# A scale vector computed by rows of matmuls instead of column tiles, behind four parked blocks

## The chip, the cores and the metric

The kernel runs on one core of a Trainium2 chip. The metric is device time in microseconds (us). The core has five engines that run side by side and wait for each other: TensorE (PE in the profile, its weight loads PEld), VectorE (DVE), ScalarE (ACT), GpSimd (POOL), and SyncE (SP), which here only issues transfers. Matmul results go to PSUM, which the kernel uses as eight banks of 128 partitions x 512 words; all else lies in SBUF.

## The reference

The reference is one attention block with adaptive layer norm, for 2 batches of 256 tokens of width 1152, in bfloat16:

```python
mod = (_silu(c) @ w_mod).reshape(B, 6, 1, D)
shift_a, scale_a, gate_a, shift_m, scale_m, gate_m = [mod[:, i] for i in range(6)]
h = _layernorm(x, axis=-1) * (1 + scale_a) + shift_a
qkv = h @ wqkv
q, k, v = qkv[..., :D], qkv[..., D:2 * D], qkv[..., 2 * D:]
p = _softmax(jnp.einsum('bqd,bkd->bqk', q, k) * D ** (-0.5), axis=-1)
a = jnp.einsum('bqk,bkd->bqd', p, v) @ wo
return x + gate_a * a
```

The change concerns `1 + scale_a`: for each of the two batches a vector of 1152 numbers, silu(c) times the columns of w_mod that belong to scale_a, and 1.

## The kernel before

The 512 tokens are four tiles of 128 (`TT`); the width is nine blocks of 128 (`KT`). The kernel centres the tokens (`centre`), turns each tile on PE so that the width lies on the partitions (`turn_firsts` for the first two of the nine blocks, into one bank; `turn_rest` for the other seven, copied to `xcT`), multiplies each block k by its part of `1 + scale_a` (`hTs`, one DVE instruction for each batch of 256 tokens), and feeds it to the K projection. The 1/std of each token is put in later, on the projected result, so the K matmuls need the scale and not the variance.

The scale vector is computed in four parts, `PA` (blocks 0, 1), `PB` (2, 3, 4), `PC` (5, 6) and `PD` (7, 8), as their weights `wS` arrive. Three of the parts are computed by rows (`scale_rows`): for each block and each of nine slices of c, one matmul with a 128x128 weight tile of `wS` and 32 columns, which are the two batches repeated; the sums fall on the partitions, where the scaling needs them. `PB` is computed by tiles (`scale_tiles`): silu(c) is the weight, 32 columns wide, and `wS` streams past; four such matmuls use four quarters of the array. The sums then lie along a row of 32 partitions, and a DVE transpose in blocks of 32 (`scale_turned`) puts them on the partitions, into `sT`. `PA` and `PB` are opened by a matmul of one row of ones (`scale_open`), which puts the 1 of `1 + scale_a` into the sum; `PC` and `PD` have it added by a DVE instruction (`scale_out`, into `s1p`).

The K projection has nine output blocks. Five of them collect in five banks (`accs`, ring `MM`) while blocks k = 0 to 8 come in (`k_row`, `k_step`; `k_row` takes some outputs in halves of 256 tokens, as the first half is scaled first). The other four, the parked ones, first take only k = 0 and 1 (`park_part`, two matmuls of 512 columns each) and are copied to `held` (`park`, on ACT or DVE); the rest is collected later (`held_block`) and added. The parked blocks, the scale parts and other small things share the three single banks `BA`, `BB`, `BC`; whoever takes a bank waits until the one before has been read out.

Each engine runs its instructions in the order in which the program writes them (`pin`). Around the change PE's order before is: the turns of tiles 0 and 1; `PA` rows for slices 0 to 3; the turn of tile 2; the first two turns of tile 3; `PA` rows for slices 4 to 8; the other turns of tile 3; K rows 0 and 1; parked block 0 (bank BA); the opening of `PB` (BC) and its tiles for slices 0 to 3; parked block 1 (BB); the tiles for slices 4 to 8; parked blocks 2 (BA) and 3 (BB); K rows 2, 3, 4. DVE in that time scales blocks 0 and 1, takes the statistics of tile 3 (`bn_part` three times and `bn_aggr`), copies parked block 1, transposes the `PB` sums and scales blocks 2, 3 and 4. ACT takes the squares of tiles 1 and 2 (`act_var`) and copies parked blocks 0, 2 and 3. POOL then makes 1/std from all four tiles' variances (`rstd`), in seven steps, and PE transposes the result (`pT3`) among the later K rows.

All instructions are recorded by one helper, so the profile gives nearly all of them line 85; they are told apart by the names of their tiles: `psS` is a scale part, `psE` a parked block, `acc` one of the five collecting banks, `tpA` and `tp` the turns, `psK` the rest of the parked blocks, `psQ` the Q projection, `ps` values, attention and output.

Of the kernel before, what the change touches and what calls it, by code (L numbers as in the profile page):

```python
# [8 lines left out]
ALU = mybir.AluOpType  # L9
AX = mybir.AxisListType  # L10
F32 = mybir.dt.float32
BF16 = mybir.dt.bfloat16
# [4 lines left out]
def kernel(  # L17
# [10 lines left out]
    P = 128  # L28
    B, N, D = x.shape
    T = B * N  # L30
    KT = D // P
# [3 lines left out]
    NCH = D // CW  # L35
# [5 lines left out]
    PA, PB, PC, PD = (0, 2), (2, 5), (5, 7), (7, KT)  # L41
    KA = PA[1]
    NR = 32
# [12 lines left out]
    const = ctx.enter_context(tc.tile_pool(name="const", bufs=1))  # L56
# [5 lines left out]
    MM, BA, BB, BC = (psum, "mm"), (psum_a, "pa"), (psum_b, "pb"), (psum_c, "pc")  # L62
# [3 lines left out]
    def bank(shape, name, dtype=None, where=None):  # L66
        if where is None:
            where = ring[turn_no[0] % len(ring)]
            turn_no[0] += 1
        return where[0].tile(shape, dtype or F32, tag=where[1], name=name)  # L70
# [21 lines left out]
    vec = _Rec(nc.vector, dve_seq)  # L92
    sca = _Rec(nc.scalar, act_seq)
    ten = _Rec(nc.tensor, pe_seq)
    spq = _Rec(nc.sync, sp_seq)
    gps = _Rec(nc.gpsimd, pool_seq)
# [10 lines left out]
    def tok(b):  # L107
        return slice(b * N, (b + 1) * N)

    def one(t):  # L110
        return slice(t * P, (t + 1) * P)

    junk = const.tile([P, 512], BF16)
# [4 lines left out]
        out=ident, in_=ident, compare_op=ALU.not_equal, fill=1.0, base=0,  # L118
# [8 lines left out]
        out=mask, in_=mask, compare_op=ALU.is_ge, fill=0.0, base=0,  # L127
# [3 lines left out]
        out=mask, in_=mask, compare_op=ALU.is_ge, fill=0.0, base=2,  # L131
# [2 lines left out]

    c_sb = const.tile([P, B, KT], BF16)
    x_sb = act.tile([P, TT, D], BF16)
    ones_row = const.tile([1, (PB[1] - PB[0]) * NR], BF16)
    gps.memset(ones_row, 1.0)
    sca.preload_act_table_set("natural_log_exp_and_others")
    sca.dma_start(out=c_sb, in_=c.rearrange("b (p k) -> p b k", k=KT))  # L140
# [4 lines left out]
    wS = wmpool.tile([P, KT, D], BF16, tag="wS")  # L145
# [60 lines left out]
    def sc_rhs(kk):  # L206
        return scT_rep[:, kk].rearrange("p r b -> p (r b)")
# [8 lines left out]
    mvs = const.tile([P, TT, 2], F32)  # L216
    snm = const.tile([P, TT], F32)
    rstd = const.tile([P, TT], F32)
    nmean = const.tile([P, TT], F32)
# [3 lines left out]
    def bn_part(t, st, s):  # L223
        vec.bn_stats(out=st[:, s, :], in_=x_sb[:, t, s * CW : (s + 1) * CW])
# [9 lines left out]
    def act_mean(t):  # L234
        sca.activation(out=xc[:, t, :], in_=x_sb[:, t, :], func=ACT.Copy, scale=-1.0 / D,
                       accum_out=nmean[:, t : t + 1])

    def act_var(t):
        sca.activation(out=xc[:, t, :], in_=x_sb[:, t, :], func=ACT.Square, bias=snm[:, t : t + 1],
                       scale=float(D) ** -0.5, accum_out=mvs[:, t, 1:2])  # L240

    def centre(t, scalar, op, c0=0, c1=D):
        vec.tensor_scalar(out=xc[:, t, c0:c1], in0=x_sb[:, t, c0:c1], scalar1=scalar, scalar2=None, op0=op)
# [5 lines left out]
    def turn_firsts(t):  # L249
        for k in range(KA):  # L250
            ten.transpose(firsts[:, k, t, :], xc[:, t, k * P : (k + 1) * P], ident)

    def turn_rest(t, where):
        rests[t] = bank([P, KT - KA, P], "tp", BF16, where)
        for k in range(KA, KT):
            ten.transpose(rests[t][:, k - KA, :], xc[:, t, k * P : (k + 1) * P], ident)

    def copy_rest(t, on_dve=False):
        evac(on_dve, xcT[:, KA:KT, one(t)], rests[t])

    def evac(on_dve, out_ap, in_ap):
        if on_dve:
            return vec.tensor_copy(out=out_ap, in_=in_ap)
        return sca.copy(out=out_ap, in_=in_ap)
# [8 lines left out]
    psS = {}  # L273

    def scale_open(part, where):
        n = part[1] - part[0]
        psS[part] = bank([P, n, NR], "psS", where=where)
        ten.matmul(psS[part].rearrange("p j r -> p (j r)"), lhsT=junk[0:1, :P], rhs=ones_row[0:1, 0 : n * NR],
                   start=True, stop=False, skip_group_check=True)

    def scale_rows(part, kk0, kk1, js=None, where=None):
        opened = part == PA
        if kk0 == 0 and not opened:
            psS[part] = bank([P, part[1] - part[0], NR], "psS", where=where)
        for j0, j1 in [part] if js is None else js:
            for kk in range(kk0, kk1):
                for j in range(j0, j1):
                    ten.matmul(psS[part][:, j - part[0], :], lhsT=wS[:, kk, j * P : (j + 1) * P], rhs=sc_rhs(kk),
                               start=(kk == 0 and j == part[0] and not opened), stop=(kk == KT - 1),
                               skip_group_check=True)  # L290

    def scale_out(part):
        vec.tensor_scalar_add(out=s1p[:, part[0] : part[1], :], in0=psS[part][:, :, 0:B], scalar1=1.0)


    wS_v = wS.rearrange("p kk (k j c) -> p kk k j c", k=KT, j=4)
    sT = const.tile([P, KT, 32], F32)

    def scale_tiles(part, kk0, kk1):
        for kk in range(kk0, kk1):  # L300
            for j in range(4):
                ten.matmul(psS[part][32 * j : 32 * j + 32], lhsT=sc_rhs(kk), rhs=wS_v[:, kk, part[0] : part[1], j, :],
                           start=False, stop=(kk == KT - 1), skip_group_check=True)

    def scale_turned(part):
        vec.transpose(out=sT[:, part[0] : part[1], :].rearrange("p k c -> p (k c)"),
                      in_=psS[part].rearrange("p k c -> p (k c)"))

    def scaled(k, sl, scalar):
        vec.tensor_scalar(out=hTs[:, k, sl], in0=xcT[:, k, sl], scalar1=scalar, scalar2=None, op0=ALU.mult)  # L310
# [6 lines left out]
    def scaled_b(k, b):  # L317
        scaled(k, tok(b), s1p[:, k, b : b + 1])

    def wk(k, f):  # L320
        return wK[:, k, f * P : (f + 1) * P]
# [8 lines left out]
    def park_part(i, where):  # L330
        parked[i] = bank([P, T], "psE", where=where)
        for k in range(KA):
            ten.matmul(parked[i], lhsT=wk(k, NACC + i), rhs=hTs[:, k, :], start=(k == 0), stop=(k == KA - 1))

    def park(i, on_dve=False):
        evac(on_dve, held[:, i, :], parked[i])
# [8 lines left out]
    def held_block(i, rows, where=None):  # L345
        if where is not None:
            psK[i] = bank([P, T], "psK", where=where)
        for k in range(*rows):
            ten.matmul(psK[i], lhsT=wk(k, NACC + i), rhs=hTs[:, k, :], start=(k == KA), stop=(k == KT - 1))
# [16 lines left out]
    sca.activation(out=xc[:, 2, 0:SPLIT], in_=x_sb[:, 2, 0:SPLIT], func=ACT.Copy, accum_out=half_a)  # L366
    vec.reduce_sum(out=half_v, in_=x_sb[:, 2, SPLIT:D], axis=AX.X)
    vec.tensor_scalar(out=nmean[:, 2:3], in0=half_v, scalar1=half_a, scalar2=-1.0 / D, op0=ALU.add, op1=ALU.mult)
    centre(2, nmean[:, 2:3], ALU.add)
    act_mean(3)  # L370
    gps.tensor_scalar_mul(out=snm[:, 1:3], in0=nmean[:, 1:3], scalar1=float(D) ** -0.5)
    for c0, c1 in ((0, KA * P), (KA * P, D)):
# [6 lines left out]
    turn_firsts(2)  # L379
    turn_rest(2, BB)  # L380
    copy_rest(2)
    turn_firsts(3)
    scale_rows(PA, 4, KT)
    turn_rest(3, BC)
    for b in range(B):
        scaled_first(0, b, psS[PA][:, 0, b : b + 1])
# [7 lines left out]
    def k_row(k, by_batch):  # L394
        for b in range(B):
            k_part(k, tok(b), 0, by_batch)
        k_part(k, slice(0, T), by_batch, NACC)
# [2 lines left out]
    k_row(1, 0)  # L400
    act_var(1)
    st3 = small.tile([P, NCH, 6], F32, tag="stats", name="stats")
    for i in range(NCH):
        bn_part(3, st3, i)
    vec.bn_aggr(out=mvs[:, 3, :], in_=st3)
    park_part(0, BA)
    park(0)
    scale_open(PB, BC)
    scale_tiles(PB, 0, 4)
    park_part(1, BB)  # L410
    park(1, on_dve=True)
    scale_tiles(PB, 4, KT)
    scale_turned(PB)
    for k in range(*PB):
        for b in range(B):
            scaled(k, tok(b), sT[:, k, b : b + 1])
    act_var(2)
    park_part(2, BA)
    park(2)
    park_part(3, BB)  # L420
    park(3)
    parts_sq = const.tile([P, P], BF16)
    gps.memset(parts_sq, 0.0)
    parts = parts_sq[:, 0 : 3 * TT].rearrange("p (t i) -> p t i", i=3)
# [8 lines left out]

    def scale_part(part):
        scale_rows(part, 0, KT, where=BB)
        scale_out(part)
        for k in range(*part):
            for b in range(B):  # L440
                scaled_b(k, b)

    k_row(PB[0], 2)
    for k in range(PB[0] + 1, PB[1]):
        k_step(k)
    held_block(0, (2, 4), BA)
    scale_part(PC)
    held_block(0, (4, 5))
    held_block(1, PB, BC)
    k_step(5)  # L450
# [4 lines left out]
    held_block(0, (5, 6))  # L455
    held_block(1, (5, 6))
    k_step(6, 0, 2)
    scale_part(PD)
    k_step(6, 2, NACC)
    bc_ps = bank([P, T], "bc_ps", where=BB)  # L460
    ten.matmul(bc_ps, lhsT=junk[:, :P], rhs=masked.rearrange("p t n -> p (t n)"), start=True, stop=True)
# [103 lines left out]
    for b in range(B):  # L565
        s_ps = bank([P, NQ, N], "s_ps")
        for i in range(NQ):
            tq = b * NQ + i
            for k in range(KT):
                ten.matmul(s_ps[:, i, :], lhsT=qkT[:, k, tq * P : (tq + 1) * P], rhs=qkT[:, KT + k, tok(b)],  # L570
                           start=(k == 0), stop=(k == KT - 1))
# [75 lines left out]
    for b in range(B):  # L647
        for gi, dv0 in enumerate(range(0, KT, 2)):
            ndv = min(2, KT - dv0)
            ps = bank([P, 2, N], "ps")  # L650
            for dd in range(ndv):
                dv = dv0 + dd
                for j in range(NQ):
                    ten.matmul(ps[:, dd, :], lhsT=v_sb[:, b * NQ + j, dv * P : (dv + 1) * P],
                               rhs=pT_sbs[b][:, j, :], start=(j == 0), stop=(j == NQ - 1))
# [3 lines left out]
    for t in range(TT):  # L659
        b = t // NQ  # L660
# [4 lines left out]
        else:  # L665
            chunks, c0 = [], 0
# [4 lines left out]
        for ci, (c0, w_) in enumerate(chunks):  # L671
# [6 lines left out]
            for k in range(KT):  # L678
                ten.matmul(
                    ps, lhsT=attnT[:, k, t * P : (t + 1) * P],  # L680
                    rhs=(wo_last[:, k, c0 - (D - TAILW) : c0 - (D - TAILW) + w_] if pregated else wO[:, k, cs]),
                    start=(k == 0 and not pregated), stop=(k == KT - 1),
# [49 lines left out]
```

## Time and profile before

| | |
|---|---|
| time, median of 3 runs | 96.34 us (96.31 to 96.38) |
| the profiled execution | 96.41 us |
| its span, first to last instruction | 94.6 us |
| PE busy | 90.1 us, 95% of the span |
| DVE busy | 69.1 us, 73% |
| ACT busy | 33.8 us, 36% |
| POOL busy | 20.8 us, 22% |
| the chain that ended last | PE 92%, DVE 4% |
| granted clock of TensorE | 1.0 |

A row of the timeline has the start and the length in us, the engine, the operation, the tiles it writes and reads, its shape, and the count of equal instructions that follow each other; in brackets stands the idle time of the engine before it and what ended it. For a matmul the first pair of numbers is the part of the array that it uses (128\*32 is 128 rows and 32 columns), then comes the shape of the data that stream past. Matmuls overlap, so a row of n matmuls lasts longer than the next one's start tells: what counts is the distance of starts. In the chain, each piece goes from the end of the one before to its own end.

### The profile page before, as it was taken

The numbers are of one execution on the slowest core, as the hardware profiler recorded it, in microseconds if no ns is written. First come the engines' busy times: TensorE is split into PE (matmuls) and PEld (weight loads), VectorE is DVE, ScalarE is ACT, GpSimd is POOL, SyncE is SP. The second block draws the span as 40 slices with busy tenths as digits, with TensorE's granted clock in tenths as the row PEclk, the third lists the DMA queues.
The fourth block names the chain that finished last, engine by engine and source line by source line (L and its number), as shares of the span: only waits on it lengthen the run. The fifth ranks groups of instructions, "written<-read, shape, count | busy, mean of one in ns | idle before, by whom it ended". The sixth has DMA issues, their size and how long they took to land.

```text
span 94.6 us, 1638 instructions
## 1 busy us (share of the span) xinstructions
PE 90.1 (95%) x641; PEld 51.7 (55%) x641; DVE 69.1 (73%) x128; ACT 33.8 (36%) x68; POOL 20.8 (22%) x26
## 2 busy tenths in 40 slices
PE   3999999999999999999999999999999999999970
PEld 1349544545445444444468656566578656565660
DVE  2497966045897999999997899990018587889880
ACT  5189975001561720093420588234246300000010
POOL 5623007200000000000000000008999990002000
PEclk9999999999999999999999999999999999999999
DMA  2999999999999999999999502200000000312212
GB/s 24 341 291 370 377 394 359 376 410 411 413 399 406 412 408 415 397 372 373 386 401 413 233 1 55 49 7 7 0 0 0 0 0 0 125 44 88 115 46 88
DMA packets 17232, 21.31 MB, mean 225 GB/s; under 512 B 2249, under 2 KB 10569, under 8 KB 17225
## 3 DMA queue, kind: packets, MB, share of 16 engines
q1 hardware_dynamic: 16809, 21.17, 61.8%
q8 instruction: 5, 0.08, 0.4%
q10 hardware_dynamic: 416, 0.04, 0.3%
q14 instruction: 2, 0.02, 0.0%
HBM read 19.76 MB, written 1.18 MB: 221 GB/s over the span
## 4 chain that ended last, share of the span: by engine, by line
PE 92%; DVE 4%; issue 0%
PE ps L85 38%; PE psQ L85 18%; PE acc L85 11%; PE psK L85 7%; PE junk_ps L85 5%; PE s_ps L85 4%; PE psS L85 2%; PE psE L85 2%; DVE o_sb L85 2%; PE tp L85 2%; DVE ga L85 2%; PE psH L85 1%; PE tpA L85 1%; DVE junk L85 1%; DVE hTs L85 0%
## 5 line engine op out<-in xcount | busy, mean ns | idle before, releaser
L85 POOL PARTITION_ALL_REDUCE gate_bc<-gacc x2 | 13.7, 6888 | 47.1 <-DVE gacc L85 47.1
L85 DVE SCALAR_TENSOR_TENSOR gacc<-wG,scT_f,gacc 128x1152 f32<-128x1152 bf16 x16 | 22.4, 1416 | 0.4
L85 PE MATMUL ps<-wV,hT 128*128 128x384 bf16 x108 | 17.7, 326 | 0.0
L85 PE MATMUL psQ<-hT,wQ 128*128 128x512 bf16 x81 | 17.6, 379 | 0.0
L85 PE MATMUL ps<-wO,attnT 128*128 128x384 bf16 (+3 forms) x108 | 17.2, 322 | 0.0
L85 PEld LDWEIGHTS <-attnT 128*128 128x128 bf16 x117 | 11.1, 98 | 6.5
L85 PEld LDWEIGHTS <-hT 128*128 128x128 bf16 x108 | 10.6, 98 | 6.9
L85 PEld LDWEIGHTS <-wQ 128*128 128x128 bf16 x81 | 7.9, 98 | 9.6
L85 PEld LDWEIGHTS <-wK 128*128 128x128 bf16 x85 | 7.8, 97 | 8.6 <-issue 1.1
L85 PE MATMUL acc<-hTs,wK 128*128 128x512 bf16 (+1 forms) x49 | 10.7, 361 | 0.0
L85 ACT CAST qkT<-psQ 128x512 bf16<-128x512 f32 x9 | 4.9, 596 | 10.6 <-PE psQ L85 10.6
L85 DVE TENSOR_TENSOR ga<-ps,gate_bc 128x384 f32<-128x384 f32 (+3 forms) x12 | 6.5, 545 | 2.8 <-PE ps L85 2.7
L85 DVE CAST attnT<-ps 128x512 bf16<-128x512 f32 (+1 forms) x6 | 3.5, 603 | 6.8 <-PE ps L85 6.8
L85 ACT CAST v_sb<-ps 128x384 bf16<-128x384 f32 x12 | 5.5, 476 | 7.9 <-PE ps L85 7.9
L85 PE MATMUL psK<-hTs,wK 128*128 128x512 bf16 x28 | 7.0, 379 | 0.0
L85 DVE TENSOR_TENSOR o_sb<-ga,x_sb 128x384 bf16<-128x384 f32 (+3 forms) x12 | 6.6, 547 | 0.4
L85 ACT CAST o_sb<-ps 128x128 bf16<-128x128 f32 x1 | 0.3, 267 | 17.3 <-PE ps L85 17.3
L85 PE MATMUL junk_ps<-junk 128*128 128x512 bf16 x11 | 4.9, 632 | 1.5 <-DVE junk L85 1.5
L85 DVE TENSOR_TENSOR hT<-hTs,held 128x512 bf16<-128x512 bf16 x9 | 5.7, 683 | 0.4 <-ACT held L85 0.4
L85 PEld LDWEIGHTS <-junk 128*128 128x128 bf16 (+1 forms) x14 | 1.8, 133 | 5.4 <-issue 3.7
L85 DVE BATCH_NORM_STATS2 stats<-x_sb 128x6 f32<-128x384 bf16 x6 | 3.0, 541 | 2.3 <-DMA x_sb<-in_x_dram 2.3
L85 PE MATMUL s_ps<-qkT 128*128 128x256 bf16 x36 | 4.1, 272 | 0.0
(82 smaller groups left out, 84.9 us busy)
## 6 DMA issues: line engine op xcount, KB each, us to landing
wG<-in_w_mod_dram SPq DMA_DIRECT2D x3, 864.0 KB, 12.0
wV<-in_wqkv_dram SPq DMA_DIRECT2D x3, 864.0 KB, 13.4
wO<-in_wo_dram SPq DMA_DIRECT2D x3, 864.0 KB, 9.0
wH<-in_w_mod_dram SPq DMA_DIRECT2D x2, 1152.0 KB, 9.5
wQ<-in_wqkv_dram SPq DMA_DIRECT2D x4, 576.0 KB, 11.7
wK<-in_wqkv_dram SPq DMA_DIRECT2D x7, 288.0 KB, 6.2
wS<-in_w_mod_dram SPq DMA_DIRECT2D x3, 320.0 KB, 6.6
x_sb<-in_x_dram SPq DMA_DIRECT2D x3, 288.0 KB, 3.4
```

The source lines that it names most:

```text
L85: r = fn(*a, **k)
```

## The change

`PB` is now computed by rows as well, and as a whole behind the four parked blocks. Its first block (2) stands alone in bank BB, opened by a matmul of the whole 128x128 array (128 rows of ones against 1/128), and is scaled straight from PSUM. Blocks 3 and 4 follow in bank BC without an opening; `scale_out` adds 1 and writes `s1p`. Parked block 2 goes to bank BC and parked block 3 to BA. ACT copies parked block 2 before it takes the squares of tile 2. DVE's third statistic of tile 3 and the aggregation stand behind the scaling of blocks 3 and 4. The centring of tile 2 is cut in two at column 512. The `PA` rows for slices 4 to 8 stand ahead of the first two turns of tile 3.

```diff
-    ones_row = const.tile([1, (PB[1] - PB[0]) * NR], BF16)
+    ones_row = const.tile([1, 2 * NR], BF16)
...
+    ones_part = const.tile([P, NR], BF16)
+    gps.memset(ones_part, 1.0 / P)
+
+    def scale_open_one(part, where):
+        psS[part] = bank([P, 1, NR], "psS", where=where)
+        ten.matmul(psS[part][:, 0, :], lhsT=junk[:, :P], rhs=ones_part, start=True, stop=False, skip_group_check=True)
+
     def scale_rows(part, kk0, kk1, js=None, where=None):
-        opened = part == PA
+        opened = part in psS
...
-    wS_v = wS.rearrange("p kk (k j c) -> p kk k j c", k=KT, j=4)
-    sT = const.tile([P, KT, 32], F32)
-
-    def scale_tiles(part, kk0, kk1):
-        for kk in range(kk0, kk1):
-            for j in range(4):
-                ten.matmul(psS[part][32 * j : 32 * j + 32], lhsT=sc_rhs(kk), rhs=wS_v[:, kk, part[0] : part[1], j, :],
-                           start=False, stop=(kk == KT - 1), skip_group_check=True)
-
-    def scale_turned(part):
-        vec.transpose(out=sT[:, part[0] : part[1], :].rearrange("p k c -> p (k c)"),
-                      in_=psS[part].rearrange("p k c -> p (k c)"))
...
-    centre(2, nmean[:, 2:3], ALU.add)
+    for c0, c1 in ((0, 4 * P), (4 * P, D)):
+        centre(2, nmean[:, 2:3], ALU.add, c0, c1)
...
+    scale_rows(PA, 4, KT)
     turn_firsts(3)
-    scale_rows(PA, 4, KT)
...
-    for i in range(NCH):
-        bn_part(3, st3, i)
-    vec.bn_aggr(out=mvs[:, 3, :], in_=st3)
+    bn_part(3, st3, 0)
+    bn_part(3, st3, 1)
+
+    def scale_part(part, where):
+        scale_rows(part, 0, KT, where=where)
+        scale_out(part)
+        for k in range(*part):
+            for b in range(B):
+                scaled_b(k, b)
+
     park_part(0, BA)
     park(0)
-    scale_open(PB, BC)
-    scale_tiles(PB, 0, 4)
     park_part(1, BB)
     park(1, on_dve=True)
-    scale_tiles(PB, 4, KT)
-    scale_turned(PB)
-    for k in range(*PB):
-        for b in range(B):
-            scaled(k, tok(b), sT[:, k, b : b + 1])
+    park_part(2, BC)
+    park(2)
     act_var(2)
-    park_part(2, BA)
-    park(2)
-    park_part(3, BB)
+    park_part(3, BA)
     park(3)
+    PB1, PB2 = (PB[0], PB[0] + 1), (PB[0] + 1, PB[1])
+    scale_open_one(PB1, BB)
+    scale_rows(PB1, 0, KT)
+    for b in range(B):
+        scaled(PB[0], tok(b), psS[PB1][:, 0, b : b + 1])
+    scale_part(PB2, BC)
+    bn_part(3, st3, 2)
+    vec.bn_aggr(out=mvs[:, 3, :], in_=st3)
...
-    scale_part(PC)
+    scale_part(PC, BB)
```

## The prediction

> **What bounds the kernel now.** I read the page first, then the chain that ended last, then the waits, and then the order of time around the edit. From the page come the span and the shares of the chain:
>
> ```profile
> span 94.6 us, 1638 instructions
> PE 92%; DVE 4%; issue 0%
> ```
>
> The chain in order of time (start, us, what) lies on the matrix engine, PE, from about 9.7 to 88.9; its longest pieces are:
>
> ```profile
> 31.13 17.48 PE psQ L85 x81
> 48.61 3.93 PE s_ps L85 x36
> 52.54 36.36 PE ps L85 x234
> ```
>
> The 81 psQ matmuls of 512 columns advance by 17.48/81 = 0.216 us each. Eight such parked matmuls (psE) need 8 x 0.216 = 1.73 us. The stretch that is changed, from the first psE matmul to the first acc matmul of row 2, is in the timeline of PE (start, us, operation):
>
> ```profile
> 11.89 0.59 PE L85 MATMUL psE<-hTs,wK 128*128 128x512 bf16 x2
> 12.42 0.21 PE L85 MATMUL psS<-ones_row,junk 1*128 1x96 bf16 x1
> 12.56 0.35 PE L85 MATMUL psS<-wS,scT_rep 128*32 128x96 bf16 x16
> 12.85 0.60 PE L85 MATMUL psE<-hTs,wK 128*128 128x512 bf16 x2
> 13.38 0.40 PE L85 MATMUL psS<-wS,scT_rep 128*32 128x96 bf16 x20
> 13.71 1.11 PE L85 MATMUL psE<-hTs,wK 128*128 128x512 bf16 x4
> ```
>
> ```profile
> 14.23 0.59 PE L85 MATMUL psE<-hTs,wK 128*128 128x512 bf16 x2
> 14.81 0.27 PE L85 MATMUL acc<-hTs,wK 128*128 128x256 bf16 x1
> ```
>
> It takes 14.81 - 11.89 = 2.92 us, so 1.19 us beside the eight matmuls. Starts tell where: two matmuls from 11.89 would let the next start at 12.32, and it starts at 12.42. Two from 12.85 end their issue at 13.28, and the tiles start at 13.38. So 0.10 us is lost each time the shape in the array (the pair behind MATMUL's names: `128*128`, `1*128`, `128*32`) changes. There are five changes, about 0.48 us. Two waits are added: the pair at 14.23 could start at 13.71 + 2 x 0.216 = 14.14 (0.08 late), and acc at 14.23 + 0.43 = 14.66 starts at 14.81 (0.15 late). The last 0.48 us is the opening matmul and the 36 tiles themselves.
>
> The waits come from these rows of VectorE (DVE), and what lies beside them on ScalarE (ACT):
>
> ```profile
> 13.49 0.69 DVE L85 COPY held<-psE 128x512 f32<-128x512 f32 x1 [0.69 <-PE psE L85]
> 14.10 0.27 DVE L85 STREAM_TRANSPOSE sT<-psS 128x96 f32<-128x96 f32 x1
> 14.47 1.26 DVE L85 TENSOR_SCALAR hTs<-xcT,sT 128x256 bf16<-128x256 bf16 x6
> ```
>
> ```profile
> 12.52 0.59 ACT L85 COPY held<-psE 128x512 f32<-128x512 f32 x1 [0.64 <-PE psE L85]
> ```
>
> The fourth block shares a bank with the second, whose copy ends at 13.49 + 0.69 = 14.18: the matmul follows 0.05 us later. The acc matmul follows the first scaling (14.47 + 0.29, below) by 0.05 us. The second block's pair ends at 12.85 + 0.60 = 13.45 and its copy starts at 13.49, so the way from PE to another engine is 0.04 us.
>
> **The change, part by part.** *Rows for tiles.* Removed are 36 tiles, one opening matmul, one transpose on DVE and the five changes of shape; added are 27 row matmuls and one opening matmul, all `128*128`. Their price is that of the third part's rows:
>
> ```profile
> 18.05 0.59 PE L85 MATMUL psK<-hTs,wK 128*128 128x512 bf16 x2
> 18.48 0.60 PE L85 MATMUL psS<-scT_rep,wS 128*128 128x32 bf16 x18
> 18.94 1.02 PE L85 MATMUL psK<-hTs,wK 128*128 128x512 bf16 x4
> ```
>
> 18 rows take 18.94 - 18.48 = 0.46 us, 0.0256 each, with no loss at either edge (18.05 + 0.43 = 18.48). So 28 of them take 0.72 us, and PE's own work falls from 0.96 to 0.72 us.
>
> *The new waits.* With all four blocks ahead, the psE matmuls start at 11.89 + n x 0.216 and are issued at 13.62. The fourth block's first one (13.19) needs ScalarE's copy of the first, 12.52 + 0.59 + 0.05 = 13.16: just in time. The opening matmul needs the bank of the second block. That block's last matmul starts at 12.54, ends 0.38 later at 12.92, DVE copies from 12.96 to 13.65, so PE opens at 13.70, 0.08 late. DVE is free by then, as one of the three statistics over tile 3 and the aggregation move behind. Ten rows from 13.70 start their last at 13.93. How long a row is in the array, and what a scaling takes, is in the answers for the tiles psS and hTs (min/median/max ns):
>
> ```profile
> L85 PE MATMUL psS<-scT_rep,wS x54: 176/176/179, 8.0 to 22.3; 128*128 128x32 bf16 x54
> ```
>
> ```profile
> L85 DVE TENSOR_SCALAR hTs<-xcT,sT x6: 277/278/285, 14.5 to 15.5; 128x256 bf16<-128x256 bf16 x6
> L85 DVE TENSOR_SCALAR hTs<-tpA,psS x2: 345/350/355, 9.3 to 9.6; 128x256 bf16<-128x256 bf16 x2
> L85 DVE TENSOR_SCALAR hTs<-tpA,s1p x2: 344/348/351, 10.0 to 10.3; 128x256 bf16<-128x256 bf16 x2
> ```
>
> The first block's sum is ready at 13.93 + 0.18 = 14.11. The scaling starts 0.04 us later as at 13.49, or 0.11: in the built program it waits for two engines by way of a separate wait instruction, and before it was so for the row at 14.47, which starts 0.10 us behind the transpose (14.10 + 0.27), where a scaling with one wait starts 0.04 behind (19.12 + 0.16 to 19.32):
>
> ```profile
> 19.12 0.16 DVE L85 TENSOR_SCALAR s1p<-psS 128x4 f32<-128x4 f32 x1 [3.38 <-PE psS L85]
> 19.32 0.87 DVE L85 TENSOR_SCALAR hTs<-xcT,s1p 128x256 bf16<-128x256 bf16 x4
> ```
>
> With 0.11 it ends at 14.22 + 0.29 = 14.51 and acc starts at 14.56; with 0.04 at 14.49. The 18 rows of the other two blocks lie beside that: their bank is the third block's, copied by ScalarE (now ahead of its squares over tile 2) from 13.35 + 0.04 for 0.59 to 13.98, so they start at 14.03 and are issued by 14.49. Both ways give acc at 14.49 or later. I take 14.55, the row with the separate wait being the nearest: 14.81 - 14.55 = 0.26 us gained, with ends at 0.25 and 0.32.
>
> The scalar now comes from PSUM. In the rows above that costs 2 ns of 350, but there the data lie in PSUM as well. Bounds: nothing, or 350 - 278 = 0.07 us for each of two scalings. I take nothing, since the scalar alone changes between those two rows; the other end is a rival.
>
> *First part's rows ahead, the centring of tile 2 in two.*
>
> ```profile
> 7.97 0.35 PE L85 MATMUL psS<-scT_rep,wS 128*128 128x32 bf16 x8
> 8.22 0.27 PE L85 MATMUL tpA<-ident,xc 128*128 128x128 bf16 x2
> ...
> 8.83 0.41 PE L85 MATMUL psS<-scT_rep,wS 128*128 128x32 bf16 x10
> 9.09 0.55 PE L85 MATMUL tp<-ident,xc 128*128 128x128 bf16 x7
> 9.69 0.38 PE L85 MATMUL acc<-hTs,wK 128*128 128x256 bf16 x2
> ```
>
> ```profile
> 7.56 0.52 DVE L85 TENSOR_SCALAR xc<-x_sb,nmean 128x1152 bf16<-128x1152 bf16 x1
> 8.27 0.65 DVE L85 TENSOR_SCALAR xc<-x_sb,nmean 128x256 bf16<-128x256 bf16 x2 [0.19 <-ACT xc L85]
> ```
>
> Eight rows from 7.97 are over at 8.18, and the transposes of tile 2 start at 8.22, behind the centring that ends at 8.08 plus a wait of two engines. With the first half done at about 7.91 that 0.04 us goes. Two pieces take 0.65 instead of 0.52 us on DVE, up to 8.21, covered by its idle time before 8.27; without that cover it would cost up to 0.13 us. The DVE scaling at 9.28 waits in the built program for the later of rows and transposes of one bank. Before that was the rows' end (9.09 - 0.026 + 0.176 = 9.24). Now it is the second transpose, which starts one transpose (0.27 of the pair less 0.22 of one, 0.055) ahead of the place of the row at 9.09, and 0.04 earlier: 8.99 + 0.22 = 9.21. PE, which starved from 9.09 + 7 x 0.055 = 9.48 to 9.69, goes on 0.03 us earlier. Bounds: -0.01 (order alone) to +0.04.
>
> *Edits that cost nothing.* The new constant on GpSimd (POOL) falls into the 0.6 us before its row at 4.23. No DMA is added or moved on SP's queue, and no weight is asked for more than 0.3 us earlier than before. The sum of tile 3's statistics comes later: DVE has the last scaling of the part at 15.7, then 0.55 and 0.24 us, 16.5, and POOL's seven steps follow (0.24 + ... as in these rows):
>
> ```profile
> 4.23 0.32 POOL L85 TENSOR_SCALAR e_sb<-e_sb 128x18 f32<-128x18 f32 x1 [0.61 <-ACT e_sb L85]
> ```
>
> ```profile
> 14.44 0.24 POOL L85 TENSOR_SCALAR rstd<-mvs 128x4 f32<-128x4 f32 x1 [6.00 <-DVE sT L85]
> ...
> 17.04 0.19 POOL L85 CAST parts_sq<-rest 128x4 bf16<-128x4 f32 x1
> ```
>
> ```profile
> 20.93 0.22 PE L85 MATMUL pT<-ident,parts_sq 128*128 128x128 bf16 x1
> ```
>
> They took 17.23 - 14.44 = 2.79 us and now end at 19.3, where PE reads them at 20.93 - 0.2 (weight load) - 0.29 = 20.4: 1.1 us to spare. The scalings of rows 3 and 4 end at 15.3 and 15.7; PE asks for them at 14.55 + 5 x 0.216 = 15.6 and 16.7.
>
> **Sum.** 0.26 + 0.03 = 0.29 us. Behind 14.8 the chain is PE alone, and the view of waits has one wait of PE's, at the start:
>
> ```profile
> PE junk_ps L85 <- DVE junk L85: 1.5, 1, 1.5
> ```
>
> so I carry the gain to the end in full. The profiled execution took 96.41 us (94.6 of span and 1.8 around it); the median is 96.34. From the profiled one 96.12, against the median 96.05. No change means within 0.2%, 0.19 us, about what a measurement can tell here.
>
> **Rivals.**
>
> *B, the scalar in PSUM slows the scaling.* Price 0.07 us on the first scaling, and then PE's third matmul of row 2 waits another 0.05 for the second: gain 0.29 - 0.12 = 0.17, 96.17. For it: these 256-column scalings take 278 ns from SBUF and 350 where PSUM is read. Against it: the two PSUM rows above do not tell the scalars apart. Beside this, the Trainium skill, VectorE: DVE Perf Modes, "Why PSUM operands drop a tier", says that any PSUM operand takes the fast mode that needs both SBUF ports away; by it B holds if the scalar counts as an operand, and no row of before has that case alone.
>
> *C, the five losses of 0.10 us belong to small matmuls and not to changes of shape, and stay at the new edges, or an event that PE does not set takes the gain back later.* Two new edges at 0.10 leave about 0.09, 96.25; a fixed event leaves nothing, 96.34. Against the first: 18.05 to 18.94 has no such loss. Against the second: all pieces behind are PE's.
>
> *D, slower: the chain from tile 3's variance to PE's transpose at 20.93.* It is 2.1 us later than before and its 2.79 us stand on POOL, whose spans are rough. PE waits if it ends after 20.4, 1.1 us later than I have it; the change loses from 1.1 + 0.29 = 1.4 us on. At twice the length (5.6 us) it would end at 22.1, cost 1.7 us and give 97.75. Against it: POOL ran these steps beside six scalings before and would now run beside an idle DVE.
>
> **How the numbers follow.** The forecast, gain 0.19 to 0.36 (both ends of the wait, both of the first part): 0.68, by itself 95.98 to 96.15. B 0.13, C 0.08. D, with every wait late enough to turn the sign, 0.11. Faster by over 0.2%: 0.68 and a little of B, 0.70. Same: the rest of B, and C, 0.19. Slower 0.11. The range takes in B and most of C: 95.95 to 96.31.
>
> **What would show it.** Right: no `128*32` matmul before psH; eight psE without a break, 1.73 us; one opening row about 0.08 us late; acc of row 2 at 14.5, 0.3 earlier than before, and every later PE piece earlier by as much. The first part is right if acc of row 0 starts at 9.65 or so. B shows as hTs<-xcT,psS at 0.35 rather than 0.28 us. D shows as an idle PE before pT. Wrong would be: a gap beside the 128x32 rows, or acc later than 14.7.

## The result and the profile after

The changed kernel takes 96.00 us (median of 22 runs, 95.85 to 96.46); the kernel before, measured beside it, 96.37 us. The ratio is 0.9958, with a 95% interval of 0.9944 to 0.9972: 0.4% faster, about 0.40 us. The profiled execution took 95.99 us, with a span of 94.2 us (before: 96.41 and 94.6).

From the page of the changed kernel, the span and the shares of the chain that ended last:

```profile
span 94.2 us, 1618 instructions
PE 84%; DMA 4%; DVE 4%; ACT 3%; issue 1%; SPq 0%
```

And pieces of that chain (start, us, what):

```profile
1.25 3.54 DMA x_sb<-in_x_dram
...
6.08 1.99 ACT xc L85 x4
...
8.10 0.27 PE tpA L85 x2
...
11.94 1.73 PE psE L85 x8
13.67 0.84 PE psS L85 x28
...
48.24 3.93 PE s_ps L85 x36
52.17 36.36 PE ps L85 x234
```

Two things are to be seen. The scores (s_ps) start at 48.24 instead of 48.61 and the last piece (ps) at 52.17 instead of 52.54: the changed kernel is 0.37 us earlier there. And the front of the chain no longer is PE's: it runs through the load of the tokens and the `xc` rows of ACT, which take the tokens' means, and PE's share fell from 92 to 84%. PE now waits for tile 2, and that matters below. The view puts this wait down to ACT, whose last such row ends at 8.07, next to PE's start at 8.10; but in a later run ("rows between and in place") PE began the same turn at 7.99 while ACT's row ended at 8.28, and both times 0.75 us behind the mean of tile 2 on DVE. So what PE waits for is the centring on DVE.

The stretch of the second part, in the timeline of PE:

```profile
11.78 1.89 PE L85 MATMUL psE<-hTs,wK 128*128 128x512 bf16 x8
13.59 0.18 PE L85 MATMUL psS<-ones_part,junk 128*128 128x32 bf16 x1
13.61 0.90 PE L85 MATMUL psS<-scT_rep,wS 128*128 128x32 bf16 x27
14.44 0.60 PE L85 MATMUL acc<-hTs,wK 128*128 128x256 bf16 x4
```

and of DVE beside it:

```profile
12.84 0.69 DVE L85 COPY held<-psE 128x512 f32<-128x512 f32 x1 [0.89 <-PE psE L85]
14.10 0.49 DVE L85 TENSOR_SCALAR hTs<-xcT,psS 128x256 bf16<-128x256 bf16 x2 [0.56 <-PE psS L85]
```

No `128*32` matmul is left here, and eight parked ones stand in one row. From the first of them to acc of row 2 it is 14.44 - 11.78 = 2.66 us, before 2.92. The rest of the gain lies in the first part. From here on I follow three distances in each trace, since they leave out when the tokens arrive, which shifts everything behind them from run to run:

- **front**: from the start of the mean of tile 2 (`nmean` on DVE) to the first turn of tile 2 (the third pair of tpA on PE);
- **turns**: from there to acc of row 0;
- **stretch**: from the first psE matmul to acc of row 2.

| us | front | turns | stretch |
|---|---|---|---|
| before | 0.915 | 1.464 | 2.923 |
| after | 0.750 | 1.471 | 2.664 |
| gain | 0.165 | -0.007 | 0.259 |

Between acc of row 0 and the first psE matmul lie 2.20 us in both. From acc of row 2 to the start of ps it is 52.54 - 14.81 = 37.73 us before and 52.17 - 14.44 = 37.73 after: all that is gained ahead of it arrives. The three add up to 0.42 us. The two profiled executions lie only 0.37 apart there because the mean of tile 2 came 0.04 us later in that of the changed kernel, at 7.35 (its row stands below) instead of 7.31, in this row of DVE in the kernel before:

```profile
7.31 0.21 DVE L85 TENSOR_SCALAR nmean<-half_v,half_a 128x1 f32<-128x1 f32 x1
```

In all 14 traces of this study the distance from acc of row 2 to ps lies between 37.72 and 37.75 us, so what a version gains in the three distances it keeps.

### The profile page after: what moved, and what is told of

Same layout as the page of the kernel before. It is cut to its first block, busy times and chain, and to the rows that moved or that the text cites. A ratio compares the mean times of both kernels' runs of the same rounds, so it can differ in the third digit from the quotient of the medians.

```text
span 94.2 us, 1618 instructions
## 1 busy us (share of the span) xinstructions
PE 89.1 (95%) x627; PEld 51.7 (55%) x632; DVE 69.2 (73%) x129; ACT 33.8 (36%) x68; POOL 21.0 (22%) x27
## 4 chain that ended last, share of the span: by engine, by line
PE 84%; DMA 4%; DVE 4%; ACT 3%; issue 1%; SPq 0%
PE ps L85 39%; PE psQ L85 18%; PE acc L85 11%; PE psK L85 6%; PE s_ps L85 4%; DMA x_sb<-in_x_dram 4%; ACT xc L85 3%; PE psS L85 2%; PE psE L85 2%; DVE o_sb L85 2%; DVE ga L85 2%; PE psH L85 1%; PE tpA L85 0%; SPq L85 0%; PE tp L85 0%
```

## The experiments

The theory: two gains on one line of PE, the removed changes of shape and tiles (second part) and the earlier turn of tile 2 (first part), and nothing lost behind. Against it stood the rivals of the prediction, and that the first part is worth nothing. Ratios are to the kernel before, measured beside each version, with 95% intervals, and can differ a little from those of the medians; most are about 0.3% wide on either side, so single terms are read from the distances and the times only bear on the sum.

### Each part alone

Second part alone is the change without these lines, first part alone is the kernel before with them:

```diff
-    centre(2, nmean[:, 2:3], ALU.add)
+    for c0, c1 in ((0, 4 * P), (4 * P, D)):
+        centre(2, nmean[:, 2:3], ALU.add, c0, c1)
...
+    scale_rows(PA, 4, KT)
     turn_firsts(3)
-    scale_rows(PA, 4, KT)
```

> The second part by rows behind the four blocks, with the centring in one piece and the first part's rows where they were. Theory S (the second part gives most, as the traces have it: from the first parked matmul to the first acc matmul of row 2 it is 2.66 us after and 2.92 before): acc of row 2 starts 0.26 us earlier than before, the time is 0.26 us shorter, 96.1, ratio 0.997. Rival F (the first part gives most): no more than 0.1 us shorter.

> The centring of tile 2 in two pieces and the first part's rows ahead, with the second part by tiles as before. Theory S: acc of row 0 starts 0.04 to 0.12 us earlier (the transposes of tile 2 start when the first piece is done, 0.12 us earlier, if PE has already got through the eight rows ahead of them; 0.04 if it has not), and the time is as much shorter, 96.25 to 96.33. Rival F: 0.2 us shorter or more, 96.15.

Second part alone: 96.11 us, ratio 0.9975 (0.9944 to 1.0007); front 0.914 and turns 1.493, which differs by up to 0.03 us between executions of one order, stretch 2.665. First part alone: 96.24 us, 0.9974 (0.9951 to 0.9997); front 0.748, turns 1.483, stretch 2.926. Each distance moves with its own part only. By the ratios the parts are worth about 0.25% each, but the interval of the second part alone reaches past 1; by the distances they are worth 0.26 (stretch) and 0.17 us (front). So the first part is not the 0.03 us that I gave it. In its trace PE, before the third pair of turns:

```profile
8.00 0.27 PE L85 MATMUL tpA<-ident,xc 128*128 128x128 bf16 x2 [0.41 <-DVE xc L85]
```

PE sat idle for 0.41 us until the centring was done, even with its first half alone.

### The two halves of the first part

Only the two-piece centring, and only the order of the rows, each in the kernel before:

```diff
-    centre(2, nmean[:, 2:3], ALU.add)
+    for c0, c1 in ((0, 4 * P), (4 * P, D)):
+        centre(2, nmean[:, 2:3], ALU.add, c0, c1)
```

> The kernel before with the centring of tile 2 in two pieces, and nothing else. If the first part's gain is this edit alone: acc of row 0 0.04 to 0.13 us earlier, 96.25 to 96.33. If it is the order of rows and transposes: nothing, 96.37.

```diff
+    scale_rows(PA, 4, KT)
     turn_firsts(3)
-    scale_rows(PA, 4, KT)
```

> The kernel before with the first part's rows for slices 4 to 8 ahead of the first two transposes of tile 3, and nothing else. The scaling of block 0 then waits for the transposes in place of the rows, 0.01 us later by the ends in the trace: no change, 96.37 to 96.38. If the order is what gives the first part's gain: 0.05 us shorter or more.

The split gives front 0.749, turns 1.463: the whole 0.165 us is its doing. The order gives front 0.917, turns 1.472: within the 0.03 us by which turns differ, nothing. The times can't show so little: 1.0007 (0.9975 to 1.0038) for the split, 0.9987 (0.9959 to 1.0016) for the order. The split's profiled execution even took 96.84 us, because the tokens came late in it; the mean of tile 2 on DVE, which no part of the change touches, started 0.64 us later than in the profile before:

```profile
7.95 0.21 DVE L85 TENSOR_SCALAR nmean<-half_v,half_a 128x1 f32<-128x1 f32 x1
```

So the worth of the split rests on the distances, on the first part alone and on the whole change, not on the times of this run.

### Why the first part is worth more: PE's rate at the start

The prediction capped this gain by the eight rows of the scale vector that stand ahead of the turn and were over at 8.18 us. They were so late because PE turned tile 0 slowly in that one execution. Before, on PE (a tile is two transposes into tpA and seven into tp):

```profile
6.47 0.39 PE L85 MATMUL tpA<-ident,xc 128*128 128x128 bf16 x2
6.67 0.95 PE L85 MATMUL tp<-ident,xc 128*128 128x128 bf16 x7
7.41 0.34 PE L85 MATMUL tpA<-ident,xc 128*128 128x128 bf16 x2
7.58 0.55 PE L85 MATMUL tp<-ident,xc 128*128 128x128 bf16 x7
```

and after, with the centring on DVE:

```profile
6.42 0.28 PE L85 MATMUL tpA<-ident,xc 128*128 128x128 bf16 x2
6.54 0.55 PE L85 MATMUL tp<-ident,xc 128*128 128x128 bf16 x7
6.93 0.28 PE L85 MATMUL tpA<-ident,xc 128*128 128x128 bf16 x2
...
7.53 0.37 PE L85 MATMUL psS<-scT_rep,wS 128*128 128x32 bf16 x8
8.10 0.27 PE L85 MATMUL tpA<-ident,xc 128*128 128x128 bf16 x2 [0.21 <-ACT xc L85]
```

```profile
7.35 0.21 DVE L85 TENSOR_SCALAR nmean<-half_v,half_a 128x1 f32<-128x1 f32 x1
7.60 0.35 DVE L85 TENSOR_SCALAR xc<-x_sb,nmean 128x512 bf16<-128x512 bf16 x1
```

In tile 0 a transpose of 128 columns advances by 0.106 us in the first ((7.41 - 6.67)/7) and by 0.056 in the second ((6.93 - 6.54)/7). The last seven of tile 1 were fast in the first as well (7.58 to the rows at 7.97 is 0.056 for each), so PE went over to the fast rate at about 7.5 us there. In the second the rows are issued by 7.53 + 8 x 0.026 = 7.74, PE waits, and the turn starts 0.15 us behind the first half of the centring (7.60 + 0.35). Of the 14 profiles taken for this study, ten have the fast rate from the first transpose on, two change to it within tile 0, and two stay slow through it: that of before, and the next one. The next one is the changed kernel with 5 instead of 11 of the matmuls on junk data by which PE is kept busy until the tokens come; their results are used nowhere, so nothing of the computation is left out.

```diff
-    fillers(11)
+    fillers(5)
```

> The changed kernel with 5 in place of 11 filler matmuls at the start (they compute nothing that is used). In the trace of before PE turned tiles 0 and 1 at 0.107 us per transpose, in that of the changed kernel at 0.056. If the first part's gain hangs on PE being through these and the eight rows before the first piece of tile 2's centring is done: with a slow start the transposes of tile 2 begin when the rows are over, 0.2 us or more later than 0.75 us behind the mean of tile 2, and the gain of the two pieces is gone. If the fillers do not set PE's pace: no difference.

One run: 96.84 us, against the median of 96.00. On PE:

```profile
6.24 0.39 PE L85 MATMUL tpA<-ident,xc 128*128 128x128 bf16 x2 [2.26 <-DVE xc L85]
6.43 0.95 PE L85 MATMUL tp<-ident,xc 128*128 128x128 bf16 x7
...
8.13 0.42 PE L85 MATMUL psS<-scT_rep,wS 128*128 128x32 bf16 x8
8.39 0.37 PE L85 MATMUL tpA<-ident,xc 128*128 128x128 bf16 x2
```

The mean of tile 2 starts at 7.32, as early as in the two profiles above, but the rows begin at 8.13 and the turn follows them at once, at 8.39: front is 1.078, so the two-piece centring gains nothing here. Turns is 2.047, as PE goes on slowly there (the rows that follow seven transposes from 8.56 start at 9.31, 0.107 for each) and goes over to the fast rate only at about 9.9 us; stretch is 2.664 as in the changed kernel. So a cap by the rows is real where PE is slow for long enough, and here it takes the whole gain. The 0.04 us of the prediction, for a change at 7.5 us, was not measured. All 14 profiles begin at the slow rate: the first four junk matmuls, of 512 columns, start 0.40 to 0.43 us apart, where the psQ matmuls of 512 columns are 0.216 apart. What differs is when PE goes over to the fast rate: in the 13 profiles with eleven junk matmuls at 4.4 to 7.5 us, and that of before is the latest of them.

### What the second part's gain consists of

First the opening: by one row of ones, as before, in place of the whole array.

```diff
-    scale_open_one(PB1, BB)
+    scale_open(PB1, BB)
```

> The changed kernel with its first block of the second part opened by one row of ones (a matmul on 1 row of the array) in place of the whole array: two changes of shape more, nothing else. If a change of shape costs 0.10 us (theory): the one into the opening is covered by its wait for the bank (0.08 us), the one out of it makes the rows 0.12 us later, acc of row 2 starts 0.12 us later than in the changed kernel, and the time is 96.1. If the losses of 0.10 us belonged to small matmuls (rival C of the prediction): no difference from the changed kernel, 96.0.

96.21 us, 0.9968 (0.9937 to 0.9998); stretch 2.784, which is 0.120 more. PE in that place:

```profile
11.82 1.89 PE L85 MATMUL psE<-hTs,wK 128*128 128x512 bf16 x8
13.65 0.18 PE L85 MATMUL psS<-ones_row,junk 1*128 1x32 bf16 x1
13.76 0.84 PE L85 MATMUL psS<-scT_rep,wS 128*128 128x32 bf16 x27
14.61 0.81 PE L85 MATMUL acc<-hTs,wK 128*128 128x256 bf16 x5
```

The way from the opening to the first row is 0.11 us where the changed kernel has 0.02. The way into the opening is 0.10 (11.82 + 1.73 = 13.55, to 13.65), but there the changed kernel waits 0.08 for its bank anyway. So a change of shape costs about 0.10 us here too, the price that I had put on each of five; for those five it rests on the gaps in the trace of before. The Trainium skill, TensorEngine Tiling (Array Packing), section Key Properties, says that a switch of the tiling mode drains TensorE, without a price; these rows agree, and give one.

Then the place: rows instead of tiles, opened by the whole array, but left where the tiles stood, between the parked blocks, and scaled straight from PSUM (`scale_open_all`, left out below with its constant, is the opening for three blocks).

```diff
...
-    scale_open(PB, BC)
-    scale_tiles(PB, 0, 4)
+    scale_open_all(PB, BC)
+    scale_rows(PB, 0, 4)
...
-    scale_tiles(PB, 4, KT)
-    scale_turned(PB)
+    scale_rows(PB, 4, KT)
...
-            scaled(k, tok(b), sT[:, k, b : b + 1])
+            scaled(k, tok(b), psS[PB][:, k - PB[0], b : b + 1])
```

> The kernel before, with only this changed: the second part is computed by rows in the two places where the tiles were (12 rows behind parked block 0, 15 behind block 1, opened by the whole array), and scaled straight from PSUM. It tells what the rows give without the move. Theory (five changes of shape at 0.10 us, and the transpose on DVE, are what is saved): eight parked matmuls 1.73 us and 28 small ones 0.72, one wait of 0.13 us for the bank of block 1, acc of row 2 at 14.46 in place of 14.81, gain 0.35 us, 96.0: more than the 0.26 us of the rows behind all four blocks. Rival (the move behind all four blocks is what gives the gain): no gain, or a loss, as PE alternates as often as before.

96.06 us, 0.9971 (0.9946 to 0.9996), without any of the first part. Stretch is 2.581: 0.342 us less than before and 0.083 less than after the change. On PE:

```profile
11.92 0.59 PE L85 MATMUL psE<-hTs,wK 128*128 128x512 bf16 x2
12.36 0.21 PE L85 MATMUL psS<-ones_part,junk 128*128 128x96 bf16 x1
12.40 0.45 PE L85 MATMUL psS<-scT_rep,wS 128*128 128x32 bf16 x12
12.70 0.59 PE L85 MATMUL psE<-hTs,wK 128*128 128x512 bf16 x2
13.13 0.53 PE L85 MATMUL psS<-scT_rep,wS 128*128 128x32 bf16 x15
13.51 1.16 PE L85 MATMUL psE<-hTs,wK 128*128 128x512 bf16 x4
14.51 0.81 PE L85 MATMUL acc<-hTs,wK 128*128 128x256 bf16 x5
```

Each piece starts where the one before is issued (11.92 + 0.43 to 12.36, 12.70 + 0.43 to 13.13); the 0.13 us that are left are a wait of parked block 3 for its bank (DVE's copy of block 1 ends at 13.33 + 0.69 = 14.02), inside the row of four. And the reverse, tiles as before but behind all four parked blocks:

```diff
...
-    scale_open_one(PB1, BB)
-    scale_rows(PB1, 0, KT)
-    for b in range(B):
-        scaled(PB[0], tok(b), psS[PB1][:, 0, b : b + 1])
-    scale_part(PB2, BC)
+    scale_open(PB, BB)
+    scale_tiles(PB, 0, KT)
+    scale_turned(PB)
+    for k in range(*PB):
+        for b in range(B):
+            scaled(k, tok(b), sT[:, k, b : b + 1])
```

> The changed kernel with the second part by tiles again, but all of it behind the four parked blocks, opened by one row, transposed on DVE and scaled from there. It has the move without the rows, three changes of shape in place of five. Theory (rows are what gives the gain): 36 tiles until 14.1, transpose until 14.6, scaling until 15.0, acc of row 2 at 15.05, 0.24 us later than before and 0.6 later than in the changed kernel: 96.6. Rival (the move is what gives it, by fewer changes of shape): acc at 14.6 or earlier, 96.2 or less.

97.01 us beside 96.60 for the kernel before, ratio 1.0022 (0.9988 to 1.0055), first part included; stretch 3.311, 0.388 us more than before. On PE, then on DVE:

```profile
13.49 0.21 PE L85 MATMUL psS<-ones_row,junk 1*128 1x96 bf16 x1
13.63 0.57 PE L85 MATMUL psS<-wS,scT_rep 128*32 128x96 bf16 x36
14.98 0.38 PE L85 MATMUL acc<-hTs,wK 128*128 128x256 bf16 x2 [0.78 <-DVE hTs L85]
```

```profile
14.25 0.28 DVE L85 STREAM_TRANSPOSE sT<-psS 128x96 f32<-128x96 f32 x1 [0.83 <-PE psS L85]
14.64 1.07 DVE L85 TENSOR_SCALAR hTs<-xcT,sT 128x256 bf16<-128x256 bf16 x5
```

Behind the parked blocks nothing covers the transpose and the scaling: PE idles 0.78 us. So it is the rows that gain (0.34 us); their move behind the blocks gives 0.08 back, and is only bearable because rows need no transpose and the first block's sum is ready after ten matmuls.

### Versions beyond the change

Rows between the turns: the `PA` rows for slices 4 to 8 and the first two turns of tile 3 go into the middle of tile 2's turns, so that the sums and the scaling are ready as the turns end (`turn_some`, left out below, turns the blocks of a tile that it is given).

```diff
...
-    turn_rest(2, BB)
-    copy_rest(2)
+    rests[2] = bank([P, KT - KA, P], "tp", BF16, BB)
+    turn_some(2, KA, KA + 4)
     scale_rows(PA, 4, KT)
     turn_firsts(3)
+    turn_some(2, KA + 4, KT)
+    copy_rest(2)
```

> The changed kernel with the first part's last ten rows and the first two transposes of tile 3 moved ahead once more, behind the sixth of tile 2's nine transposes. PE is idle for 0.22 us before acc of row 0, as it waits for the scaling of block 0, which waits for these two. With them three transposes (0.165 us) earlier, acc of row 0 starts at 9.41 in place of 9.575 if the scaling alone holds it, and all behind is 0.165 us earlier: 95.84. If a bank, a weight (the second half of the first part's weights had landed at 8.36 in the trace of before) or ScalarE holds it as well: 0.05 us or less.

96.28 us beside 96.60, ratio 0.9962 (0.9928 to 0.9997); turns 1.305 instead of 1.471, the stretch 2.665 as after. The distance gained 0.166 us, but the time didn't show it: in the profiled execution the tokens were late (mean of tile 2 at 8.05), and the runs spread from 95.89 to 97.02, with a single one at 98.58. Then all of it together: rows in the old places, the two-piece centring, the rows between the turns, and parked block 1 copied by ACT instead of DVE.

```diff
-    park(1, on_dve=True)
+    park(1)
```

> What gave the gains put together on the kernel before: the second part by rows in its old two places; the centring of tile 2 in two pieces; the first part's last rows and tile 3's first two transposes behind the sixth of tile 2's transposes; and parked block 1 copied by ScalarE, so that its bank comes free 0.1 us earlier. By the traces so far: 0.165 us from the centring, 0.165 from the transposes, 0.34 from the rows in place, 0.1 from the copy, 0.8 us in all, 95.6, if the pieces behind acc of row 2 still start as far behind it as in all runs so far. If the weights set a floor (the third part's second half landed at 17.45 us in the trace of before and 17.95 in that of the rows in place, and would be asked for at about 17.7): some of it comes back as a wait ahead of the third part's rows or of psH, 95.7 to 95.9.

The same with that copy left on DVE, and the change itself once more beside them:

> The same, with parked block 1 copied by DVE as before. From the first parked matmul to acc of row 2 it should take 2.58 us as with the rows in place, against 2.45 with the copy on ScalarE; the time is 0.1 us longer than with it, if nothing behind absorbs it.

> The changed kernel beside the two others on one chip: 96.0, ratio to before 0.996, as measured.

| | median, us | ratio (95%) | front | turns | stretch |
|---|---|---|---|---|---|
| rows between and in place | 95.91 | 0.9928 (0.9900 to 0.9955) | 0.750 | 1.491 | 2.473 |
| the same, copy on DVE | 95.90 | 0.9942 (0.9914 to 0.9970) | 0.750 | 1.487 | 2.582 |
| the change again | 95.97 | 0.9934 (0.9904 to 0.9965) | 0.749 | 1.472 | 2.664 |

The first has the lowest ratio of all kernels run, but the three intervals overlap. It is better than the kernel before; whether it is better than the changed one is open: by the distances it is 0.17 us ahead of it, by the medians 0.06. Of the 0.8 us that I expected over the kernel before, the distances hold 0.59 and the medians 0.53 (96.44 to 95.91). The copy on ACT is worth 0.109 us of stretch, the place 0.082. The order between the turns, worth 0.166 us in the run before, gave nothing here. On PE of the first of them, and from the profile's view of wS (what was waited for, us in all, times):

```profile
8.10 0.39 PE L85 MATMUL tp<-ident,xc 128*128 128x128 bf16 x4
8.49 0.42 PE L85 MATMUL psS<-scT_rep,wS 128*128 128x32 bf16 x10
```

```profile
  DMA wS<-in_w_mod_dram: 0.4, 2
```

Four transposes from 8.10 are issued at 8.32, and the rows start at 8.49: PE's weight loads waited twice, 0.4 us in all, for the scale's weights to arrive: ahead of the first rows of this part, and here. Rows that are asked for earlier meet the transfer. In the run where the order did pay, the mean of tile 2 came 0.8 us later (8.05, here 7.24), and PE had no wait for the weights.

## Why the prediction was right, and where not

**The forecast.** 96.05 us against a measured 96.00, with a gain of 0.29 us against 0.40. The likeliest case came about, but the sum was short by one term, and that the time fell near the forecast is in part luck. The gain of 0.40 us (0.27 to 0.54 by the interval, 0.42 by the distances) lies beyond the 0.36 that was the upper end of the forecast (its lower end, 0.19, is the limit of what counts as a change; the ends of its own terms add up to 0.24). The time is inside the range of 95.95 to 96.31 by 0.05, of which 0.03 is that the kernel before took 96.37 this time, not 96.34.

**Rows for tiles, the five changes of shape.** Held. In the changed kernel the way into the opening is 0.08 us, the wait for its bank, and from there to the rows 0.02; one opening of another shape costs 0.12 us; rows in the old place gain 0.342, where the terms of the sum that apply there (0.24 of PE's own work and 0.10 less of waiting) make 0.34.

**The new waits.** Held to a hundredth. The eight psE end their issue at 11.78 + 1.73 = 13.51, and PE opens at 13.59, 0.08 late, as I had it; DVE's copy of the second parked block ends at 12.84 + 0.69 = 13.53. I put acc 2.66 us behind the first psE, and it is 2.66. The scaling with two waits starts 0.11 us behind the sums, the end of the bounds that I took: the last of the first block's nine rows starts at 13.61 + 8 x 0.0256 = 13.81, 0.18 later the sum is there, 13.99, and DVE starts at 14.10.

**The scalar from PSUM (rival B).** Refuted by the profile's view of hTs in the changed kernel (min/median/max ns):

```profile
L85 DVE TENSOR_SCALAR hTs<-xcT,s1p x4: 281/282/286, 14.7 to 15.3; 128x256 bf16<-128x256 bf16 x4
L85 DVE TENSOR_SCALAR hTs<-xcT,psS x2: 284/288/291, 14.1 to 14.3; 128x256 bf16<-128x256 bf16 x2
```

With the scalar in PSUM and the data in SBUF the scaling takes 288 ns, with both in SBUF 282: not 350. With the rows in place, six scalings with the scalar in PSUM take 283 to 286. The sentence of the Trainium skill, VectorE: DVE Perf Modes, "Why PSUM operands drop a tier", that any PSUM operand caps the mode, does not hold for the scalar operand of this instruction; the measurement decides.

**Losses at small matmuls, or a gain taken back (rival C).** Both refuted: 27 rows and their opening go through at 0.026 us each, but for one wait of 0.07 us for the bank of blocks 3 and 4, and the 37.73 us behind acc of row 2 are the same.

**The late chain on POOL (rival D).** Refuted. POOL, and PE that reads from it:

```profile
16.52 0.23 POOL L85 TENSOR_SCALAR rstd<-mvs 128x4 f32<-128x4 f32 x1 [8.12 <-DVE mvs L85]
...
19.05 0.24 POOL L85 CAST parts_sq<-rest 128x4 bf16<-128x4 f32 x1
```

```profile
20.57 0.22 PE L85 MATMUL pT<-ident,parts_sq 128*128 128x128 bf16 x1
```

The chain starts at 16.5 and takes 2.77 us, the forecast to a few hundredths, and PE comes for it 1.1 us later (20.57 less 0.2 for the weight load, less 19.29).

**The first part.** This is the step that was wrong: "Eight rows from 7.97 are over at 8.18 ... that 0.04 us goes", with bounds -0.01 and +0.04. The mechanism was the right one, the earlier half of the centring, but the term was 0.165 us, four times the upper bound. The rows that capped it were late because of PE's slow start in the one execution that I had; I took its PE times as the kernel's own, though the transposes that I quoted from 8.22 on ran at 0.055 us, those of tile 0 took nearly twice that (0.106), and nothing in the kernel's text makes them differ. (What I expected of fewer fillers names tiles 0 and 1 as slow; it was tile 0 and the first transpose of tile 1.) The 0.01 us for the order is too little to be told from the 0.03 by which turns differ. The extra time of the two pieces on DVE was covered, as I had it. acc of row 0 stood at 9.57, not 9.65.

**What stays open.** That the first part's 0.165 us is there in the time is shown by sums (first part alone, 0.9974, and the whole), while the split alone gave no measurable change in time. And why PE goes over to its fast rate at 4.4 us in one execution and at 7.5 in another is seen but not explained by these runs; that fewer fillers put it off, to 9.9, rests on one run.

## What to carry to other kernels

A cap that rests on when an engine was done in one profiled execution is only as good as that engine's rate there: compare equal instructions within the trace, and if they run at two rates, work the term out at both. Count the changes of array shape in a short stretch on PE; each cost about 0.10 us here, as much as four matmuls of 32 columns over the whole array. And where the arrival of data shifts a whole run, read the gain from distances within the trace, because times with intervals of 0.3% cannot tell 0.17 us.

## What was not expected of the hardware

PE's transposes of tile 0 ran at 0.107 us each in two executions, and at 0.056 in most, while in these two the granted clock is 9 tenths or more in all slices of the profile and its mean is 1.0:

```profile
PEclk9999999999999999999999999999999999999999
```

The Trainium skill, TensorE: Matmul & The Clock Gate, in Part 1 on the HAM clock gate, gives 106.7 ns for 128 columns while the array is cold and 55.6 once warm, and says that the moment of warming differs from run to run because its window runs free. The rates here are these two, and the moment differs here as well, by 3 us between executions with the same fillers; the profile's own row of the clock does not show it.

A scalar read from PSUM by a DVE scaling of SBUF data costs at most 6 ns of 282, by the medians of two and four. And a centring cut in two, 0.13 us longer in all on DVE, makes the kernel's front 0.165 us shorter.
